# Merging the scores of one attention unit with the outputs of the unit before, and bringing output weights back as whole words

## The chip, the cores and the metric

The kernel runs on one core of a Trainium2 chip. The metric is the device time of one execution in microseconds (us); the median of three runs of the kernel before is 892.08 us. The engines are TensorE (PE in the rows), VectorE (DVE), ScalarE (ACT), GpSimd (POOL) and SyncE (SP), which here only issues transfers.

## The reference

A decayed attention without softmax (retention) is followed by two feed-forward layers over 2304 tokens of width 512:

```python
scores = scale * np.matmul(q, k.transpose(0, 1, 3, 2))     # 4 batches, 8 heads, 576 positions, 64 wide
ret = scores * Dmat                                        # gamma**(i-j) for i >= j, else 0
x = np.matmul(ret, v)                                      # then reshaped to 2304 x 512
h = x @ w_in                                               # 512 -> 2048
x = (h / (1 + np.exp(-1.702 * h))) @ w_out                 # 2048 -> 512
xn = x / np.sqrt(np.mean(x * x, -1) + 1e-6) * rms_g
g = xn @ w_gate                                            # 512 -> 1536
out = (g / (1 + np.exp(-g)) * (xn @ w_val)) @ w_out2       # 1536 -> 512
```

## The kernel before

Every float32 operand of a large matmul is held as two parts: a rounded high part and the remainder, the low part. A product is three matmuls (`three`, L277): high by high, high by low, low by high. The low part of the weight is first needed by the third matmul of each three.

The first feed-forward layer takes the tokens in five blocks of 512, 384, 384, 512 and 512 (blocks 0 to 4), each in 16 steps `f`. A step has an *up* part (`m1_up`, 12 matmuls into a buffer `h`; there are two such buffers, `ps_h`), after which ScalarE applies the activation (L621) and rounds it (L601) and VectorE subtracts to get the low part (L603), and a *down* part (`m1_down`, 12 matmuls into four accumulators). The down part of step `f` is placed two steps later, after the up part of that step (`LAG = 2`, the list `pending`). So TensorE usually sees up(f), down(f-2), up(f+1), down(f-1), and so on.

The attention is computed in units of 128 tokens, 18 of them. Units 0 to 3 come at the start; units 4 to 17 are put between the steps of blocks 0 to 3, in time for the block that needs them. A unit has three phases, each placed in front of an up part: `a_trans` (8 transposes of k and q), `a_scores` (32 small matmuls for the scores, up to 32 for the carried state; 64 by 64 tiles of the array) followed by `a_state` on VectorE, and `a_out` (32 small matmuls for scores by v and up to 32 for the carried state by q; the same tile size). `a_out` leaves its result in two PSUM buffers of the pool `ps_at`; ScalarE copies them (L479), VectorE adds (L483), and the function `parts` is put on the list `rows`. It is run inside the same step's `m1_up`, behind the rounding of the activation: ScalarE rounds x (L489) and GpSimd subtracts (L490).

`attend` also issues the loads of the next unit: the load of unit u+1 is issued at the transposes of unit u (SyncE queue), into the lowest free slots of 512 words (`wslots`). `a_decay` scales v on GpSimd.

The output weights: in block 0 and 1 fourteen of the sixteen rows (`NKEEP = 14`) lie on chip as whole float32 words, and `w_rot` makes the two parts for each step (ScalarE L268, VectorE L269) in one of three buffers. In block 1 both parts are stored to DRAM (512 KB, L272). From block 2 on `w_rot` loads the two parts back, ready for use (512 KB, ScalarE's queue, L274).

Blocks 1 to 4 also carry work for the second layer on ScalarE, VectorE, GpSimd and SyncE (`make`: gate and value weights are joined, combined, split and stored, L189, L190, L243, L834, L861 to L863; sums for the norm). All engines run their instructions in the order in which the program issues them (`manual_schedule`).

Of the kernel before, what the change touches and what calls it, by code (L numbers as in the profile page):

```python
# [24 lines left out]
NSLOT = 22  # L25
# [7 lines left out]
def block_of(t):  # L33

    n = 0
    while t >= BLOCKS[n]:
        t -= BLOCKS[n]
        n += 1
    return n, t
# [3 lines left out]
def kernel(  # L43
# [46 lines left out]
    scrap = dram.tile([1, 16], F32, name="scrap")  # L90
    qrow = dram.tile([1, H * 128], F32, name="qrow")
    srow = dram.tile([1, H], F32, name="srow")
    out_d = dram.tile([NF1, 128, 1024], F32, name="out_d")
    up_d = dram.tile([7 * NF2, 128, 512], F32, name="up_d")


# [61 lines left out]
    def w_free(key, f):  # L158
        give(W.pop((key, f))[0])
# [97 lines left out]
                low() if rest is None else rest.append(low)  # L257

    R = {}

    def w_rot(n, f):


        at = A_ROT + (n * NF1 + f) % 3 * 1024
        both, wh, wl = fast[:, at:at + 1024], fast[:, at:at + 512], fast[:, at + 512:at + 1024]
        if ("out", f) in W:
            w = W["out", f][1]
            nc.scalar.copy(out=wh, in_=w)  # L268
            nc.vector.tensor_tensor(out=wl, in0=w, in1=wh.bitcast(F32), op=ALU.subtract)  # L269
            if n == 1 or f >= NKEEP:  # L270
                w_free("out", f)
                to_store.append(lambda: nc.sync.dma_start(out=out_d[f], in_=both.bitcast(F32)))  # L272
        else:
            nc.scalar.dma_start(out=both.bitcast(F32), in_=out_d[f])  # L274
        R["out", f] = (wh, wl)

    def three(ps, lhs, rhs, first, last, more=False):  # L277
# [38 lines left out]
    def a_tile(u, name):  # L316

        aslots[u, name], t = w_slot() if wfree else half_slot()
        return t

    def a_free(u, *names):
        for nm in names:
            give(aslots.pop((u, nm)))

    def a_load(u, what="kqv"):
        (b, s), (b1, _) = units[u]
        for nm in what:
            t = a_tile(u, nm).rearrange("p (h d) -> p h d", h=H)
            a = {"k": k, "q": q, "v": v}[nm]

            sides = [(slice(0, H), slice(0, H))] if nm == "v" else [
                (slice(j, H, 2), slice(HP * j, HP * j + HP)) for j in range(2)
            ]
            for to, of in sides:
                if b == b1:
                    nc.sync.dma_start(out=t[:, to], in_=a[b, of, s:s + 2 * C, :].rearrange("h p d -> p h d"))
                else:
                    for c, (bc, sc) in enumerate(units[u]):
                        nc.sync.dma_start(
                            out=t[C * c:C * c + C, to], in_=a[bc, of, sc:sc + C, :].rearrange("h p d -> p h d")  # L340
                        )
            raws[u, nm] = t
# [5 lines left out]
    def a_decay(u):  # L348
        vr = raws[u, "v"]
        nc.gpsimd.tensor_tensor(  # L350
            out=vr, in0=vr, in1=vdec.unsqueeze(2).to_broadcast([128, H, D]), op=ALU.mult
        )

    def a_trans(u, where):
        kr, qr = (raws[u, nm] for nm in "kq")
        pt = a_psum(where)

        more = ps_acc.tile([128, 512], F32, tag="acc", name="at") if u == 0 else pt[0]
        for i, t in ((1, kr), (0, qr)):
            for p in range(HP):  # L360
                nc.tensor.transpose(  # L361
                    (more if i == 0 and p > 1 else pt[i])[:, p * 128:(p + 1) * 128],
                    t[:, 2 * p:2 * p + 2, :].rearrange("p h d -> p (h d)"),
                    ident,
                )
        qT = a_tile(u, "qT")
        kT = a_tile(u, "kT")
        nc.scalar.copy(out=kT, in_=pt[1])
        if u > 3:
            nc.vector.tensor_tensor(out=qT, in0=pt[0], in1=qdec, op=ALU.mult)  # L370
        elif u == 0:
            nc.vector.tensor_copy(out=qT[:, :256], in_=pt[0][:, :256])
            nc.scalar.copy(out=qT[:, 256:], in_=more[:, 256:])
        else:
            nc.scalar.copy(out=qT, in_=pt[0])
        if u < 5:
            a_decay(u)
        a_free(u, "q")
        st[u] = tuple(t.rearrange("p (a c) -> p a c", c=128) for t in (qT, kT))
# [4 lines left out]

    def a_scores(u, where):
        qT, kT = st[u]
        sc = a_psum(where)
        for p in range(HP):  # L390
            for c in range(2):
                for j in range(2):
                    hs, cs = slice(64 * j, 64 * j + 64), slice(C * c, C * c + C)
                    nc.tensor.matmul(  # L394
                        sc[j][cs, p * C:(p + 1) * C], kT[hs, p, cs], qT[hs, p, cs], start=True, stop=True
                    )
        kr, vt = raws[u, "k"], raws[u, "v"]
        for p in range(HP):
            for j in range(2):
                for c in range(2):  # L400
                    if goes_on(u, c):
                        hs, cs = slice(64 * j, 64 * j + 64), slice(C * c, C * c + C)
                        nc.tensor.matmul(  # L403
                            sc[c][hs, (HP + p) * D:(HP + p + 1) * D], kr[cs, 2 * p + j, :], vt[cs, head(p, j), :],
                            start=True, stop=True,
                        )
        r = [a_tile(u, f"r{j}").rearrange("p (a c) -> p a c", c=128)[:, :, :C] for j in range(2)]
        for j in range(2):
            nc.vector.tensor_tensor(
                out=r[j], in0=sc[j][:, :HP * C].rearrange("p (a c) -> p a c", c=C),  # L410
                in1=mask.unsqueeze(1).to_broadcast([128, HP, C]), op=ALU.mult,
            )
        st[u] = (qT, r, sc)
        a_free(u, "kT", "k")

    def a_state(u, chunks=(0, 1)):

# [590 lines left out]
    with tc.manual_schedule():  # L1008
# [1 line left out]
        AT = (ps_at.__enter__(), "at")  # L1010
        ACC = (ps_acc, "acc")

        per_block = {}
        for u in range(len(units)):
            per_block.setdefault(block_of(2 * C * u)[0], []).append(u)
        phases = [(fn, u) for n in range(1, N1) for u in per_block[n] for fn in (a_trans, a_scores, a_out)]

        to_load = [("in", 0), ("in", 1)]
        for f in range(NF1):
# [178 lines left out]
        load()  # L1198
        late = list(range(6, len(units)))

        def attend(phases):
            for fn, u in phases:
                fn(u, AT)
                if fn is a_out and u + 1 < len(units):
                    a_decay(u + 1)
                if fn is a_scores:
                    a_state(u)
                if fn is a_trans and u > 4 and late:
                    a_load(late.pop(0))

        pending, spread = [], []

        def run(todo, k):
            for _ in range(min(k, len(todo))):
                todo.pop(0)()
# [16 lines left out]
        own = NSLOT - 13  # L1232
        x = None
        for n in range(N1):
            todo = [t for t in phases if t[1] in per_block.get(n + 1, [])]
            gap = {}
            for i, t in enumerate(todo):
                at = 1 + i * (NF1 - 2) // max(1, len(todo))
                gap.setdefault((2, 3, 5, 6, 8, 10, 11, 12, 14)[i] if n == 0 else at, []).append(t)
            last = n == N1 - 1  # L1240
            if n == 2:
                assert not set(range(own, own + 2)) - set(wfree), wfree
# [15 lines left out]
                FILL["parts"] = wslots[:, 14 * TH:20 * TH]  # L1258
            for f in range(NF1):
                if n == 0:  # L1260
                    attend(gap.get(f, []))
                    if f == 2:
                        conv_next(2)
                    if f > 0:
                        w_rot(n, f - 1)
                    if f > 1:
                        conv_next(2)
                if n == 1 and f == 0:
                    nc.sync.dma_start(out=rg, in_=rms_g.rearrange("(k p) -> p k", p=128))
                if n == 1 and f == 11:  # L1270
                    w_rot(n, f - 1)
                    assert wfree[-11:] == list(range(own + 2, NSLOT)), wfree
                    del wfree[-11:]
                    FILL["made"] = [wslots[:, i * 512:i * 512 + 512] for i in range(own + 6, own + 1, -1)]
                    FILL["sums"] = wslots[:, (NSLOT - 6) * 512:(NSLOT - 4) * 512]
                    FILL["gate"], FILL["val"] = (wslots[:, (NSLOT - i) * 512:(NSLOT - i + 1) * 512] for i in (4, 3))
                    sfree.append(NSTG)
# [21 lines left out]
                if n == 1 and 0 < f < NKEEP + 1 and f != 11:  # L1299
                    w_rot(n, f - 1)  # L1300
                if n > 0:
                    attend(gap.get(f, []))
                    if n > 1 or f >= NKEEP:
                        w_rot(n, f)
                if (n, f) == (0, 0):


                    m1_up(n, f, lambda: conv_join([to_conv.pop(0)]), lambda: conv_words(*to_conv[0]))
                else:
                    m1_up(n, f, lambda: run(rows, 1))  # L1310
                run(to_store, len(to_store))
                if norm:
                    spread = norm.popleft() + spread
# [20 lines left out]
                w_rot(n, NF1 - 1)  # L1334
        run(to_store, len(to_store))
        assert not made and not parts_of
        run(down(pending.pop(0)), KD)
        sfree.extend((NSTG + 1, NSTG + 2))
        chunks = []
# [124 lines left out]
```

## Time and profile before

| | |
|---|---|
| runs | 891.97, 892.08, 892.97 us (median 892.08) |
| the profiled execution's own time | 893.62 us |
| its span in the profile | 891.5 us (2.1 us lie around it) |
| TensorE busy | 882.4 us, 99% of the span, 6170 matmuls |
| VectorE, ScalarE, GpSimd busy | 509.9, 384.4, 83.8 us |
| transfers | 192.96 MB, mean 216 GB/s |

A wait of TensorE lengthens the execution one for one while TensorE is the engine that is never idle; the other engines' idle time costs nothing by itself. Matmuls are pipelined: the time that one takes is read from the distance of the starts, not from its own length.

### The profile page before, as it was taken

The numbers are of one execution on the slowest core, as the hardware profiler recorded it, in microseconds if no ns is written. First come the engines' busy times: TensorE is split into PE (matmuls) and PEld (weight loads), VectorE is DVE, ScalarE is ACT, GpSimd is POOL, SyncE is SP. The second block draws the span as 40 slices with busy tenths as digits, with TensorE's granted clock in tenths as the row PEclk, the third lists the DMA queues.
The fourth block names the chain that finished last, engine by engine and source line by source line (L and its number), as shares of the span: only waits on it lengthen the run. The fifth ranks groups of instructions, "written<-read, shape, count | busy, mean of one in ns | idle before, by whom it ended". The sixth has DMA issues, their size and how long they took to land.

```text
span 891.5 us, 16172 instructions
## 1 busy us (share of the span) xinstructions
PE 882.4 (99%) x6170; PEld 794.1 (89%) x6170; DVE 509.9 (57%) x920; ACT 384.4 (43%) x767; POOL 83.8 (9%) x95
## 2 busy tenths in 40 slices
PE   8999999999999999999999999999999999999998
PEld 7788889999999888888889999999999999999997
DVE  4787644454584457445744557766565666344444
ACT  3796644365545534454453344334323215122222
POOL 2200101122232212211200000000000000000000
PEclk9999999999999999999999999999999999999999
DMA  9985435489999976779597676557655556555553
GB/s 221 266 262 186 131 117 191 145 267 330 301 294 319 289 238 196 277 275 330 205 312 267 207 263 212 167 155 238 223 153 157 155 157 219 175 157 163 166 165 106
DMA packets 153131, 192.96 MB, mean 216 GB/s; under 512 B 66204, under 2 KB 94112, under 8 KB 153056
## 3 DMA queue, kind: packets, MB, share of 16 engines
q1 hardware_dynamic: 145268, 165.32, 59.4%
q10 hardware_dynamic: 7660, 26.36, 8.8%
q8 instruction: 49, 0.80, 0.3%
q0 software_dynamic: 128, 0.27, 0.2%
q14 instruction: 26, 0.21, 0.1%
HBM read 149.70 MB, written 42.21 MB: 215 GB/s over the span
## 4 chain that ended last, share of the span: by engine, by line
PE 97%; DVE 1%; ACT 1%; DMA 0%; issue 0%; SPq 0%; DVEq 0%; ACTq 0%
PE h L280 18%; PE h L282 17%; PE h L281 17%; PE acc L281 11%; PE acc L282 11%; PE acc L280 11%; PE v L282 2%; PE v L281 2%; PE v L280 2%; PE at L361 2%; PE at L470 2%; PE at L394 1%; PE at L403 1%; PE at L506 1%; DMA wslots<-in_q_dram 0%; PE at L563 0%
## 5 line engine op out<-in xcount | busy, mean ns | idle before, releaser
L280 PE MATMUL h<-fast 128*128 128x384 f32 (+1 forms) x824 | 291.5, 354 | 1.6 <-DVE S L535 1.1
L282 PE MATMUL h<-fast 128*128 128x384 f32 (+1 forms) x824 | 287.3, 349 | 0.0
L281 PE MATMUL h<-fast 128*128 128x384 f32 (+1 forms) x824 | 286.9, 348 | 0.1
L911 DVE TENSOR_TENSOR wslots<-h,wslots 128x384 f32<-128x384 f32 x180 | 100.2, 557 | 151.3 <-PE h L282 151.0
L282 PE MATMUL acc<-fast 128*128 128x512 f32 (+1 forms) x464 | 174.4, 376 | 0.0
L281 PE MATMUL acc<-fast 128*128 128x512 f32 (+1 forms) x464 | 174.2, 375 | 0.0
L280 PE MATMUL acc<-fast 128*128 128x512 f32 (+1 forms) x464 | 173.5, 374 | 0.0
L280 PEld LDWEIGHTS h<-fast 128*128 128x128 f32 x824 | 154.7, 188 | 13.2 <-ACT fast L215 1.5
L281 PEld LDWEIGHTS h<-fast 128*128 128x128 f32 x824 | 154.8, 188 | 9.0 <-issue 0.3
L282 PEld LDWEIGHTS h<-fast 128*128 128x128 f32 x824 | 154.6, 188 | 7.7
L603 DVE TENSOR_TENSOR fast<-g,fast 128x512 fp32r<-128x512 f32 (+1 forms) x80 | 56.2, 703 | 123.8 <-ACT fast L601 123.6
L944 ACT CAST fast<-g 128x384 fp32r<-128x384 f32 x36 | 18.6, 517 | 220.4 <-DVE g L914 220.4
L621 ACT ACTIVATE g<-h 128x512 f32<-128x512 f32 (+1 forms) x80 | 44.4, 555 | 142.9 <-PE h L282 140.3
L282 PEld LDWEIGHTS acc<-fast 128*128 128x128 f32 x464 | 87.1, 188 | 13.2
L281 PEld LDWEIGHTS acc<-fast 128*128 128x128 f32 x464 | 87.1, 188 | 12.1
L280 PEld LDWEIGHTS acc<-fast 128*128 128x128 f32 x464 | 87.1, 188 | 12.0
L601 ACT CAST fast<-g 128x512 fp32r<-128x512 f32 (+1 forms) x80 | 46.4, 580 | 2.5
L834 POOL TENSOR_TENSOR wslots<-wslots 128x256 f32<-128x256 f32 x48 | 40.3, 860 | 74.2 <-DVE wslots L243 54.3
L862 DVE TENSOR_TENSOR wslots<-wslots 128x256 fp32r<-128x256 f32 x84 | 39.7, 502 | 13.1 <-ACT wslots L861 12.9
L189 ACT ACTIVATE sslots<-sslots 128x512 f32<-128x512 f32 x55 | 37.0, 674 | 4.8 <-DMA sslots<-in_moe_w_gate_dram 4.6
L190 ACT ACTIVATE sslots<-sslots 128x512 uint32<-128x512 uint8 x55 | 36.5, 663 | 0.0
L861 ACT CAST wslots<-wslots 128x256 fp32r<-128x256 f32 x84 | 30.8, 401 | 11.9 <-DVE wslots L243 8.6
(136 smaller groups left out, 857.4 us busy)
## 6 DMA issues: line engine op xcount, KB each, us to landing
fast<-up_d SPq DMA_DIRECT2D x252, 256.0 KB, 3.1
fast<-out_d ACTq DMA_DIRECT2D x50, 512.0 KB, 5.5
up_d<-wslots SPq DMA_DIRECT2D x84, 256.0 KB, 5.1
sslots<-in_moe_w_out_dram SPq DMA_DIRECT2D x20, 512.0 KB, 5.3
out_d<-fast SPq DMA_DIRECT2D x16, 512.0 KB, 3.8
sslots<-in_moe_w_in_dram SPq DMA_DIRECT2D x15, 512.0 KB, 5.2
sslots<-in_moe_w_gate_dram SPq DMA_DIRECT2D x11, 512.0 KB, 6.4
sslots<-in_moe_w_val_dram SPq DMA_DIRECT2D x10, 512.0 KB, 7.0
```

What stands on the lines that cost most here:

```text
L189: nc.scalar.activation(out=hi, in_=hi, func=AF.Prelu, scale=2.0 ** -112, alpha=-(2.0 ** 32))
L190: nc.scalar.activation(out=lo, in_=byte, func=AF.Copy, scale=1 / 32, bias=-31 / 64)
L280: nc.tensor.matmul(ps, lh, rh, start=first, stop=False, skip_group_check=more)
L281: nc.tensor.matmul(ps, lh, rl, start=False, stop=False, skip_group_check=more)
L282: nc.tensor.matmul(ps, ll, rh, start=False, stop=last, skip_group_check=more)
L601: nc.scalar.copy(out=gh, in_=g)
L603: nc.vector.tensor_tensor(out=gl, in0=g, in1=gh.bitcast(F32), op=ALU.subtract)
L621: nc.scalar.activation(out=g, in_=ps, func=AF.Gelu_apprx_sigmoid)
L834: nc.gpsimd.tensor_tensor(out=o, in0=a, in1=b, op=op)
L861: nc.scalar.copy(out=wh.bitcast(F32R), in_=w)
L862: nc.vector.tensor_tensor(out=wl.bitcast(F32R), in0=w, in1=wh, op=ALU.subtract)
L911: nc.vector.tensor_tensor(out=o, in0=a, in1=b, op=ALU.add)
```

## The change

- The scores of unit u and the outputs of unit u-1 become one phase, `a_both`, for units 8 to 17. The outputs then go to the two buffers of `ps_h` instead of `ps_at`. A step with such a phase is *joined*: the down part that would follow the up part is put in front of it. `a_decay` of unit u moves to its transposes, the load of unit u+1 to `a_both` of unit u.
- The places of the phases are written out by hand (`at_steps`). Joined steps are 4, 7, 10 of block 1; 2, 6, 10, 14 of block 2; 3, 7, 9 of block 3.
- Of the fourteen kept output weights the whole word is stored in block 1 (256 KB, straight from its slot, without waiting for the parts). From block 2 on the word is loaded (256 KB) and halved on chip by `w_halve`, called behind `m1_up`: in step f it halves the weight of step f-1.

```diff
+    def w_halve(f=-1):
+        while whole and whole[0][0] != f:
+            _, wh, wl = whole.popleft()
+            nc.scalar.copy(out=wh, in_=wl.bitcast(F32))
+            nc.vector.tensor_tensor(out=wl, in0=wl.bitcast(F32), in1=wh.bitcast(F32), op=ALU.subtract)
...
-            if n == 1 or f >= NKEEP:
+            if f >= NKEEP:
                 w_free("out", f)
-                to_store.append(lambda: nc.sync.dma_start(out=out_d[f], in_=both.bitcast(F32)))
+                to_store.append(lambda: nc.sync.dma_start(out=both_d[f - NKEEP], in_=both.bitcast(F32)))
+            elif n == 1:
+                nc.sync.dma_start(out=out_d[f], in_=w)
+                w_free("out", f)
+        elif f >= NKEEP:
+            nc.scalar.dma_start(out=both.bitcast(F32), in_=both_d[f - NKEEP])
         else:
-            nc.scalar.dma_start(out=both.bitcast(F32), in_=out_d[f])
+            nc.scalar.dma_start(out=wl.bitcast(F32), in_=out_d[f])
+            whole.append((f, wh, wl))
...
-        if u < 5:
+        if u < 5 or u > 7:
             a_decay(u)
...
+        def a_both(u, where):
+            a_scores(u, where, True)
+            a_out(u - 1, HID)
+            a_state(u)
...
+        phases += [(a_trans, 7), (a_scores, 7)]
+        phases += [(fn, u) for u in range(8, len(units)) for fn in (a_trans, a_both)]
+        phases.append((a_out, len(units) - 1))
+        at_steps = (
+            (2, 3, 5, 6, 8, 10, 11, 12, 14),
+            (0, 1, 2, 4, 5, 7, 8, 10),
+            (0, 2, 4, 6, 8, 10, 12, 14),
+            (1, 3, 5, 7, 9, 11, 13),
+        )
...
+            if late and (fn is a_both or fn is a_trans and 4 < u < 8):
+                a_load(late.pop(0))
+            return fn is a_both
...
+                if joined:
+                    run(down(pending.pop(0)), KD)
                 if (n, f) == (0, 0):
...
                     m1_up(n, f, lambda: run(rows, 1))
+                w_halve(f)
                 run(to_store, len(to_store))
```

## Rows read from the trace of the kernel before

**Rows 1.** The page, busy time of the engines (us, share of the span, instructions).

```profile
PE 882.4 (99%) x6170; PEld 794.1 (89%) x6170; DVE 509.9 (57%) x920; ACT 384.4 (43%) x767; POOL 83.8 (9%) x95
```

**Rows 2.** Busy time by stretch: blocks 2 and 3, with granted clock and DMA share.

```profile
201.50:282.80 81.30, 81.30 (x900) 78.12 (x900) 51.16 (x99) 42.07 (x95) 23.61 (x24) 1.00 0.98 309
282.80:372.30 89.50, 89.50 (x868) 74.04 (x867) 49.81 (x94) 42.18 (x89) 18.27 (x19) 1.00 0.79 248
```

**Rows 3.** Timeline of TensorE, steps of 384 columns (start, duration, line, operation).

```profile
197.35 0.33 PE L280 MATMUL acc<-fast 128*128 128x384 f32 x1
...
201.51 0.33 PE L280 MATMUL acc<-fast 128*128 128x384 f32 x1
...
206.55 0.33 PE L280 MATMUL acc<-fast 128*128 128x384 f32 x1
...
208.73 0.69 PE L394 MATMUL at<-wslots 64*64 64x64 f32 x32
209.24 0.65 PE L403 MATMUL at<-wslots 64*64 64x64 f32 x32
...
212.01 0.33 PE L280 MATMUL acc<-fast 128*128 128x384 f32 x1
...
264.40 0.33 PE L280 MATMUL acc<-fast 128*128 128x384 f32 x1
...
267.09 0.41 PE L470 MATMUL at<-wslots,S 64*64 64x64 f32 x16
...
269.63 0.33 PE L280 MATMUL acc<-fast 128*128 128x384 f32 x1
```

**Rows 4.** Timeline of TensorE, a step of 512 columns.

```profile
380.44 0.39 PE L280 MATMUL h<-fast 128*128 128x512 f32 x1
...
383.16 0.39 PE L280 MATMUL acc<-fast 128*128 128x512 f32 x1
```

**Rows 5.** Timeline of four engines behind the up part after unit 7's outputs.

```profile
141.20 0.69 DVE L269 TENSOR_TENSOR fast<-wslots,fast 128x512 fp32r<-128x512 f32 x1
...
144.87 0.33 PE L280 MATMUL acc<-fast 128*128 128x384 f32 x1
...
145.07 0.49 ACT L621 ACTIVATE g<-h 128x384 f32<-128x384 f32 x1 [1.57 <-PE h L282]
...
146.02 0.62 ACT L489 CAST fast<-x 128x512 fp32r<-128x512 f32 x1
...
146.54 0.62 ACT L268 CAST fast<-wslots 128x512 fp32r<-128x512 f32 x1
...
146.71 1.28 POOL L490 TENSOR_TENSOR fast<-x,fast 128x512 fp32r<-128x512 f32 x1 [12.46 <-ACT fast L489]
...
147.19 1.35 DVE L269 TENSOR_TENSOR fast<-wslots,fast 128x512 fp32r<-128x512 f32 x1 [0.49 <-ACT fast L268]
```

**Rows 6.** Timeline of ScalarE and GpSimd at the same place in block 3.

```profile
301.68 0.60 ACT L621 ACTIVATE g<-h 128x512 f32<-128x512 f32 x1 [2.29 <-PE h L282]
...
303.53 1.30 POOL L490 TENSOR_TENSOR fast<-x,fast 128x512 fp32r<-128x512 f32 x1 [8.34 <-ACT fast L489]
```

**Rows 7.** Timeline of ScalarE and VectorE: evacuating the outputs of units 7 and 12.

```profile
142.85 0.65 ACT L479 COPY x<-at 128x256 f32<-128x256 f32 x2 [1.68 <-PE at L470]
143.60 0.49 DVE L483 TENSOR_TENSOR x<-at,x 128x128 f32<-128x128 f32 x2 [1.71 <-ACT x L479]
...
251.83 0.38 ACT L479 COPY x<-at 128x256 f32<-128x256 f32 x1 [1.53 <-PE at L470]
...
254.41 0.48 DVE L483 TENSOR_TENSOR x<-at,x 128x128 f32<-128x128 f32 x2
```

**Rows 8.** SyncE's queue and landing times: the load of unit 9 (KB each, us to landing).

```profile
142.34 1.66 SPq L336 DMA_DIRECT2D wslots<-in_k_dram  x2
144.10 1.55 SPq L336 DMA_DIRECT2D wslots<-in_q_dram  x2
...
wslots<-in_q_dram SPq DMA_DIRECT2D x2, 128.0 KB, 4.4
```

More of the change, by code (lines that the diff above doesn't have):

```diff
@@ L92 @@
     srow = dram.tile([1, H], F32, name="srow")
-    out_d = dram.tile([NF1, 128, 1024], F32, name="out_d")
+    out_d = dram.tile([NKEEP, 128, 512], F32, name="out_d")
+    both_d = dram.tile([NF1 - NKEEP, 128, 1024], F32, name="both_d")
     up_d = dram.tile([7 * NF2, 128, 512], F32, name="up_d")
@@ L259 @@
     R = {}
+    whole = deque()
+    def w_halve(f=-1):
[3 more added lines that the diff above has]
+            nc.vector.tensor_tensor(out=wl, in0=wl.bitcast(F32), in1=wh.bitcast(F32), op=ALU.subtract)
     def w_rot(n, f):
@@ L383, in goes_on, with a_scores @@
         return units[u][c][1] + C < S
-    def a_scores(u, where):
+    def a_scores(u, where, over=False):
         qT, kT = st[u]
@@ L406, in a_scores @@
                         )
+        if over:
+            a_free(u, "kT", "k")
         r = [a_tile(u, f"r{j}").rearrange("p (a c) -> p a c", c=128)[:, :, :C] for j in range(2)]
@@ L413, in a_scores @@
         st[u] = (qT, r, sc)
-        a_free(u, "kT", "k")
+        if not over:
+            a_free(u, "kT", "k")
     def a_state(u, chunks=(0, 1)):
@@ L1011 @@
         ACC = (ps_acc, "acc")
[L1013 to L1016, printed above, removed]
+        HID = (ps_h, "h")
+        def a_both(u, where):
+            a_scores(u, where, True)
+            a_out(u - 1, HID)
+            a_state(u)
+        phases = [(fn, u) for u in range(4, 7) for fn in (a_trans, a_scores, a_out)]
+        phases += [(a_trans, 7), (a_scores, 7)]
+        phases += [(fn, u) for u in range(8, len(units)) for fn in (a_trans, a_both)]
+        phases.append((a_out, len(units) - 1))
+        at_steps = (
[4 rows of a table added]
+        )
+        gap = {(n, f): phases.pop(0) for n, steps in enumerate(at_steps) for f in steps}
+        assert not phases
         to_load = [("in", 0), ("in", 1)]
@@ L1199, with attend @@
         late = list(range(6, len(units)))
[L1201 to L1209, printed above, removed]
+        def attend(n, f):
+            if (n, f) not in gap:
+                return False
+            fn, u = gap[n, f]
+            fn(u, AT)
+            if fn is a_out and u < 7:
+                a_decay(u + 1)
+            if fn is a_scores:
+                a_state(u)
+            if late and (fn is a_both or fn is a_trans and 4 < u < 8):
+                a_load(late.pop(0))
+            return fn is a_both
         pending, spread = [], []
@@ L1234 @@
         for n in range(N1):
[L1235 to L1239, printed above, removed]
             last = n == N1 - 1
@@ L1260 @@
                 if n == 0:
-                    attend(gap.get(f, []))
+                    joined = attend(n, f)
                     if f == 2:
@@ L1271 @@
                     w_rot(n, f - 1)
-                    assert wfree[-11:] == list(range(own + 2, NSLOT)), wfree
+                    assert wfree[-11:] == list(range(own + 2, NSLOT)), (wfree, aslots, [(k, W[k][0]) for k in W if k[0] == "out"])
                     del wfree[-11:]
@@ L1301 @@
                 if n > 0:
-                    attend(gap.get(f, []))
+                    joined = attend(n, f)
                     if n > 1 or f >= NKEEP:
                         w_rot(n, f)
+                if joined:
+                    run(down(pending.pop(0)), KD)
                 if (n, f) == (0, 0):
@@ L1336 @@
         assert not made and not parts_of
+        w_halve()
         run(down(pending.pop(0)), KD)
```

## The prediction

> **What bounds the kernel.** I read the page first: TensorE is busy 99% of the span [rows 1]. The table by stretch shows that in blocks 2 and 3, where most of the change lies, TensorE has no idle time at all, at a granted clock of 1.00, while VectorE is busy 51 of 81 us and ScalarE 42, and the DMA engines are nearly full in block 2 (share 0.98) [rows 2]. So time can only be saved by giving TensorE less to do, and any new wait of TensorE is paid in full. Fewer bytes or less work elsewhere are worth nothing by themselves. Then I read TensorE's timeline, for what a phase costs between two steps, and the timelines of the other engines behind one up part, for when a product of theirs is ready.
>
> **Part 1: ten phases fewer.** Two plain steps, 12 up and 12 down matmuls, take 201.51 - 197.35 = 4.16 us. With a scores phase of 64 small matmuls between, the same stretch takes 212.01 - 206.55 = 5.46: the phase costs 1.30. Unit 13's outputs have 48 small matmuls (32 and the 16 of the row): 269.63 - 264.40 = 5.23, so 1.07 [rows 3]. Sixteen small matmuls are 0.23, 64 are 0.92, and 0.38 us is a fixed cost of going into and out of a phase of 64 by 64 tiles. `a_both` has the same matmuls as the two phases that it replaces, in one tile size, so it saves one fixed cost: 10 units, 3.8 us. The other bound is 0, if 128 small matmuls in a row run slower than 64; no row has so many. I take 3.8, since L403's 32 begin 0.51 us after the first of the scores' 32, 16 ns for each, with nothing lost between the two [rows 3].
>
> **Part 2: halving on chip, in ordinary steps.** 42 weights (14 in each of three blocks) get a ScalarE copy and a VectorE subtract. The nearest rows are the same operations on the same shapes in block 1: 0.62 us (L268) and 0.69 us (L269) [rows 5]. In an ordinary step the halving of weight f-1 stands behind up(f), and down(f-1) comes after down(f-2) and up(f+1), 4.16 us later or 5.44 in the wider blocks: cost nothing, hidden by these two. 26 and 29 us more on ScalarE and VectorE fit into their idle time [rows 2].
>
> **Part 3: halving in a joined step.** Here the cover is gone. Down(f-2) has been put in front of up(f), so after up(f) TensorE goes straight to up(f+1) and then to down(f-1). Between the end of up(f) and the first use of weight f-1 lies one up part: 2.08 us at 384 columns (half of 4.16), 2.72 at 512 (383.16 - 380.44 [rows 4]). The low part is needed by the third matmul, two twelfths of a part later: 2.43 and 3.17 us after the end of up(f).
>
> When is it ready? Behind up(f) ScalarE has, in order, the activation, its rounding, the rounding of x (L489, because the outputs of a unit were made in this very step), and only then the copy of `w_halve`. Block 1 of the kernel before shows exactly this row of work. Up ends where the next dense matmul starts, 144.87; the activation starts at 145.07, the rounding of x at 146.02, the copy L268 runs from 146.54 to 147.16, and VectorE's L269 starts at 147.19. But it takes 1.35 us instead of 0.69, because GpSimd's L490, released by the rounding of x, runs from 146.71 to 147.99; L269 ends 0.55 us behind it, at 148.54 [rows 5]. So the low part is ready 148.54 - 144.87 = 3.67 us after the end of up(f). In the kernel before that cost nothing, for its use was further off.
>
> In block 2 TensorE then waits 3.67 - 2.43 = 1.24 us in each of four joined steps. In block 3 the activation starts at 301.68, so up ended 0.20 before, at 301.48, and GpSimd starts at 303.53, 2.05 us after the end against 146.71 - 144.87 = 1.84: everything is 0.21 later [rows 5, 6]. 3.88 - 3.17 = 0.71 us in each of three. The sum is 4 x 1.24 + 3 x 0.71 = 7.1 us. The lower bound is that VectorE is not held up by GpSimd: ready 0.66 earlier, so 0.58 and 0.05, sum 2.5. An upper bound of 9 adds some 0.27 each for a chain that starts late. Block 1's joined steps have no halving behind the up part.
>
> On the hold-up, the Trainium skill says under "Who interferes with whom" on the page "SBUF — State Buffer" that VectorE with two SBUF inputs and a GpSimd instruction that reads SBUF exclude each other, and that the one that issues first wins. The row agrees (1.35 against 0.69, ending behind GpSimd). By the rule a VectorE that issues first would bring the sum to the lower bound; the rows have GpSimd first, by 147.19 - 146.71 = 0.48 us.
>
> **Part 4: outputs in the up buffers.** Up(f) needs the buffer that VectorE's add of L483 reads last. For unit 7 the add ends at 144.09, 1.24 us after the copies began [rows 7], and the down part put in front covers 2.08. For unit 12 it is 254.89 - 251.83 = 3.06 us, since VectorE was behind: 1.0 us over the cover [rows 7]. Of the four joined steps in block 2 I count half of one such case: 0.5 us, with bounds 0 and 4.
>
> **Part 5: loads issued later.** In block 1 the load of units 9 and 10 is now issued at the end of the joined phase, and the transposes stand one step later. By the order in which slots are freed, k takes the slot of the transposed q of the unit whose outputs were just made, so it can't start before the phase ends. Cover: one down, one up and four transposes of k, some 4.6 us. Unit 9's load before took from 142.34 to the second issue of q, about 144.88, plus 4.4: 6.9 us [rows 8]. So a wait of up to 2.3 us each; but half the bytes of the weights' stores are gone and the queue is free by then. I take 0.5 each, 1.0 in all, bounds 0 and 4.6. In blocks 2 and 3 two steps, at least 8.3 us, cover 6.9.
>
> **At nothing:** the whole-word stores wait for no parts, but a slot is now free only when its store has read it; units 7, 9 and 10 get such a slot for a tile first used two steps later, some 8 us. The decay of v on GpSimd comes two steps ahead of its use. 42 x 256 KB less to load shortens no wait that TensorE has.
>
> **Sum.** -3.8 + 7.1 + 0.5 + 1.0 = +4.8 us. Against the profiled execution's 893.62 that is 898.4; the median of the runs is 1.54 lower, so 896.9 us.
>
> **Rivals.** (a) The saving stays, and the kernel is faster. Mechanism: the rounding of x is not ahead of the halving in the joined step. Then the copy starts where L489 did, 146.02 - 144.87 = 1.15 us after up, and the low part is there at about 2.5: 0.1 over in block 2, nothing in block 3. It decides below 2.43 us. With loads in time: 892.1 - 3.8 + 0.4 + 0.5 = 889.2. For it: ScalarE is idle half the time in block 2 [rows 2]. Against it: the code runs x's rounding in the same step's up part. 0.13.
>
> (b) VectorE is not held up: -3.8 + 2.5 + 0.5 + 1.0 = +0.2, 892.3, no change. For it: GpSimd is only 0.48 us ahead. Against: L269 in rows 5. 0.17.
>
> (c) A second wait beside the halving: loads at their bound give 3.6 more, 900.5; evacuation at its bound 3.5 more, 900.4; a merged phase that saves nothing 3.8 more, 900.7. 0.10 together. For evacuation the Trainium skill, "TensorEngine Tiling (Array Packing)", section "PSUM Bottleneck", warns that small tiles speed up the matmuls and not the emptying of PSUM, which may become the limit. By that rule the time is the 900.4 of this case; of four outputs in block 2 one was late.
>
> **Numbers.** My forecast, the wait for the halved weight in seven joined steps, has 0.60 and gives 896.9. A measurement of this kernel tells about 0.2%, 1.8 us, from no change. Faster is (a) and a little of (b): 0.14. Same is most of (b) and the edge of the forecast: 0.16. Slower is the rest: 0.70. The range leaves out (a) and the upper half of (c): 890.8 to 900.5; the forecast's own, with its unknown waits, is 894 to 900.
>
> **What would show it.** In the profile after, TensorE should wait 7 times, in front of the third or first matmul of a down part into `acc`, for VectorE at the subtract of `w_halve`, 1.2 us each in block 2 and 0.7 in block 3; none in block 4, which has halving but no joined steps. A phase of 128 small matmuls should cost 2.2 us. Waits of the transposes of units 9 and 10 for k or q, or of an up part for L483 in a joined step, would show parts 4 and 5. I am wrong if VectorE's subtract ends within 2.4 us of the up part, or if phases cost the same merged.

## The result, and the profile after

The kernel is slower by a little under 1%: 900.49 us (median of 4 runs, 899.66 to 901.69) against 892.53 (4 runs), ratio 1.0085 with a 95% interval of 1.0072 to 1.0099. The profiled execution has a span of 899.3 us. One place in the description of the change has to be put right: by `at_steps` the joined steps of block 3 are 3, 7 and 11, not 3, 7 and 9. There are three of them either way, all with a weight to halve.

First the page of the changed kernel: busy times, the shares of the chain that ended last, and the group of third matmuls of the down parts. The last line is the same group in the kernel before.

```profile
PE 880.9 (98%) x6170; PEld 791.2 (88%) x6170; DVE 540.9 (60%) x962; ACT 404.3 (45%) x809; POOL 89.0 (10%) x95
...
PE 90%; ACT 3%; DVE 3%; DMA 2%; issue 1%; SPq 0%; POOL 0%; ACTq 0%; DVEq 0%; POOLq 0%
...
L297 PE MATMUL acc<-fast 128*128 128x512 f32 (+1 forms) x464 | 175.1, 377 | 4.3 <-DVE fast L268 4.3
...
L282 PE MATMUL acc<-fast 128*128 128x512 f32 (+1 forms) x464 | 174.4, 376 | 0.0
```

TensorE has the same 6170 matmuls as in [rows 1] and is busy 1.5 us less, yet the span is 7.8 us longer: the time went into waits. L297 is the third matmul of `three` in the changed file (L282 before, where it never waited); L268 is the subtract of `w_halve`. The table of TensorE's waits names them (in total, times, longest):

```profile
PE acc L297 <- DVE fast L268: 4.3, 6, 0.8
PE h L751 <- DVE fast L734: 2.2, 2, 1.9
...
PE h L295 <- DMA fast<-up_d: 0.9, 1, 0.9
PE at L376 <- DMA wslots<-in_q_dram: 0.7, 2, 0.6
...
PE h L295 <- DVE x L501: 0.4, 1, 0.4
```

The table counts only the time in which TensorE was empty. What a wait costs is read from the starts. This is a joined step of block 2 in the changed kernel, its 128 small matmuls and then the first use of the halved weight, in the timeline of four engines:

```profile
207.44 0.33 PE L295 MATMUL acc<-fast 128*128 128x384 f32 x1
...
209.62 0.69 PE L409 MATMUL at<-wslots 64*64 64x64 f32 x32
...
211.06 0.65 PE L488 MATMUL at<-wslots,S 64*64 64x64 f32 x32
...
213.83 0.33 PE L295 MATMUL h<-fast 128*128 128x384 f32 x1
...
217.05 0.62 ACT L507 CAST fast<-x 128x512 fp32r<-128x512 f32 x1
...
217.57 0.61 ACT L267 CAST fast<-fast 128x512 fp32r<-128x512 f32 x1
...
217.75 1.29 POOL L508 TENSOR_TENSOR fast<-x,fast 128x512 fp32r<-128x512 f32 x1 [9.69 <-ACT fast L507]
...
218.22 1.36 DVE L268 TENSOR_TENSOR fast<-fast 128x512 fp32r<-128x512 f32 x1 [0.48 <-ACT fast L267]
...
218.24 0.44 PE L295 MATMUL acc<-fast 128*128 128x384 f32 x1
...
218.52 0.33 PE L296 MATMUL acc<-fast 128*128 128x384 f32 x1
...
219.64 0.45 PE L297 MATMUL acc<-fast 128*128 128x384 f32 x1 [0.79 <-DVE fast L268]
...
219.92 0.34 PE L295 MATMUL acc<-fast 128*128 128x384 f32 x1
```

Two down parts and the phase between them take 213.83 - 207.44 = 6.39 us, 2.23 more than the 4.16 of two plain parts: a merged phase costs 2.23 us, where two phases cost 1.30 each [rows 3]. So 0.37 us per merged phase is saved, 3.7 in all. Added up over all of them, the starts say the same: 21 phases of units 7 to 17 take 26.8 us before, the 11 that are left take 23.1. Then the up part that began at 213.83 ends 2.08 later, at 215.91, a second up part follows at once, and the down part should begin at 217.99. It begins at 218.24, waiting for the high part; its third matmul, due 0.35 us after 217.99, comes at 219.64, for VectorE's subtract ended at 219.58, 3.67 us after the end of the up part. The third begins 0.06 us after the subtract's end, and the matmul behind it comes 0.28 us later instead of 0.17. The two parts together take 1.4 us more than they would.

The same chain in step 3 of block 3, where the up part ends at 310.45 and the subtract at 312.98 + 1.36 = 314.34, 3.89 us later; this one costs 0.86 us:

```profile
310.45 0.39 PE L295 MATMUL h<-fast 128*128 128x512 f32 x1
...
312.98 1.36 DVE L268 TENSOR_TENSOR fast<-fast 128x512 fp32r<-128x512 f32 x1 [0.35 <-ACT fast L267]
...
314.39 0.50 PE L297 MATMUL acc<-fast 128*128 128x512 f32 x1 [0.59 <-DVE fast L268]
```

The second row of the table of waits was not foreseen. In block 3 the joined step 7 has no wait at the halving, since TensorE waits somewhere else before it, in the sums of the norm (two matmuls against a matrix of ones, L750 and L751). The timeline there:

```profile
338.31 1.29 POOL L508 TENSOR_TENSOR fast<-x,fast 128x512 fp32r<-128x512 f32 x1 [19.27 <-ACT fast L507]
...
338.79 1.36 DVE L268 TENSOR_TENSOR fast<-fast 128x512 fp32r<-128x512 f32 x1 [0.35 <-ACT fast L267]
...
338.98 0.33 PE L750 MATMUL h<-fast,ones 128*128 128x384 f32 x1
...
340.07 1.08 DVE L734 TENSOR_TENSOR fast<-ssq,fast 128x384 fp32r<-128x384 f32 x1
...
341.20 0.44 PE L751 MATMUL h<-fast,ones 128*128 128x384 f32 x1 [1.89 <-DVE fast L734]
```

GpSimd's subtract holds up the halving's subtract, and that the low part of the norm's sum, which stands behind it on VectorE; the second matmul of the sums comes 2.2 us after the first instead of 0.2. The low part of the sum (L734) itself takes 1.08 us here, beside GpSimd's next instruction, against 0.55 at the sums of block 2 in the same run.

The whole stretch of the first layer, from the up part that waits for the carried state near the start to the first up part of the second layer, leaves out the start, which differs from execution to execution (that up part begins anywhere from 29.8 to 33.6 us). It took 470.57 - 31.88 = 438.7 us before and 477.81 - 30.82 = 447.0 after: 8.3 longer. By the distances of the starts: phases -3.7; halving 4 x 1.4 + 2 x 0.86 = 7.3; sums 2.7; unit 10's q 0.7; an evacuation 0.6; together 7.6. The other 0.7 is not assigned; a halving 0.2 late in an ordinary step is part of it.

### The profile page after: what moved, and what is told of

Its sections match the earlier page's. It is cut to its first block, busy times and chain, and to the rows that moved or that the text cites. A ratio compares the mean times of both kernels' runs of the same rounds, so it can differ in the third digit from the quotient of the medians.

```text
span 899.3 us, 16209 instructions
## 1 busy us (share of the span) xinstructions
PE 880.9 (98%) x6170; PEld 791.2 (88%) x6170; DVE 540.9 (60%) x962; ACT 404.3 (45%) x809; POOL 89.0 (10%) x95
## 4 chain that ended last, share of the span: by engine, by line
PE 90%; ACT 3%; DVE 3%; DMA 2%; issue 1%; SPq 0%; POOL 0%; ACTq 0%; DVEq 0%; POOLq 0%
PE h L295 16%; PE h L297 16%; PE h L296 16%; PE acc L297 11%; PE acc L295 10%; PE acc L296 10%; PE v L297 2%; PE v L296 2%; PE v L295 2%; PE at L376 1%; PE at L488 1%; DMA fast<-up_d 1%; DVE fast L268 1%; PE at L409 1%; PE at L418 1%
## 5 line engine op out<-in xcount | busy, mean ns | idle before, releaser
L297 PE MATMUL h<-fast 128*128 128x384 f32 (+1 forms) x824 | 287.2, 349 | 0.0
L297 PE MATMUL acc<-fast 128*128 128x512 f32 (+1 forms) x464 | 175.1, 377 | 4.3 <-DVE fast L268 4.3
L297 PEld LDWEIGHTS h<-fast 128*128 128x128 f32 x824 | 154.7, 188 | 7.7
L297 PEld LDWEIGHTS acc<-fast 128*128 128x128 f32 x464 | 87.1, 188 | 20.1 <-DVE fast L268 6.8
L852 POOL TENSOR_TENSOR wslots<-wslots 128x256 f32<-128x256 f32 x48 | 44.7, 950 | 79.7 <-DVE wslots L244 59.8
L880 DVE TENSOR_TENSOR wslots<-wslots 128x256 fp32r<-128x256 f32 x84 | 36.7, 467 | 6.5 <-ACT wslots L879 6.3
L508 POOL TENSOR_TENSOR fast<-x,fast 128x512 fp32r<-128x512 f32 x14 | 18.3, 1304 | 222.3 <-ACT fast L507 222.3
L268 DVE TENSOR_TENSOR fast<-fast 128x512 fp32r<-128x512 f32 x42 | 38.0, 904 | 3.3 <-ACT fast L267 3.3
```

What stands on the lines that cost most here:

```text
L268: nc.vector.tensor_tensor(out=wl, in0=wl.bitcast(F32), in1=wh.bitcast(F32), op=ALU.subtract)
L297: nc.tensor.matmul(ps, ll, rh, start=False, stop=last, skip_group_check=more)
L852: nc.gpsimd.tensor_tensor(out=o, in0=a, in1=b, op=op)
L880: nc.vector.tensor_tensor(out=wl.bitcast(F32R), in0=w, in1=wh, op=ALU.subtract)
```

## The experiments

Each ratio is to runs of the kernel before that were taken beside the run, whose medians lie between 892.0 and 892.6 us. The last column is from one profiled execution each; where its mean granted clock was under 0.999 it stands beside it, and a part of the length is then that of the lower clock.

| run | us (median, runs) | ratio to the kernel before (95%) | first layer's stretch, us |
|---|---|---|---|
| before | 892.53 (4) | | 438.7 |
| changed | 900.49 (4) | 1.0085 (1.0072 to 1.0099) | 447.0 |
| e1 merged phases, no halving | 892.91 (12) | 1.0007 (0.9991 to 1.0023) | 438.6 |
| e2 halving, phases as before | 893.28 (12) | 1.0005 (0.9994 to 1.0017) | 438.9 |
| e3 halving first in joined steps | 893.02 (12) | 1.0000 (0.9988 to 1.0012) | 440.1 |
| e4 x's subtract issued later | 902.34 (4) | 1.0106 (1.0081 to 1.0132) | 449.2 (clock 0.996) |
| e5 e3, sums and unit 10 moved | 891.92 (12) | 0.9995 (0.9982 to 1.0007) | 438.4 (clock 0.997) |
| e6 x's subtract on VectorE, later | 895.81 (4) | 1.0041 (1.0026 to 1.0055) | 441.7 |
| e7 down part behind again | 905.08 (4) | 1.0140 (1.0127 to 1.0153) | 450.2 (clock 0.998) |
| e8 halving before x | 895.45 (4) | 1.0033 (1.0020 to 1.0046) | 442.1 |
| e9 e5, halving first everywhere | 890.78 (12) | 0.9985 (0.9973 to 0.9998) | 437.9 |
| e10 e1, sums and unit 10 moved | 891.01 (12) | 0.9987 (0.9973 to 1.0001) | 438.6 |

The theory: in joined steps the cover between the halving and its use (the work of TensorE that stands between the two) is one part instead of two, and the weight is late. Rivals: halving costs wherever it stands; merging itself costs.

**e1: merged phases alone.** `w_rot` as in the kernel before, so both parts are stored and loaded.

```diff
-            nc.scalar.dma_start(out=wl.bitcast(F32), in_=out_d[f])
-            whole.append((f, wh, wl))
+            nc.scalar.dma_start(out=both.bitcast(F32), in_=out_d[f])
```

> The changed kernel, but both parts of the output weights are stored and loaded back as in the kernel before; no halving on chip. If the late halved weight is the cause (theory): the saving of ten phases (3.7 us) stays and only the late load of unit 10 (0.7) and one late evacuation (0.5) stand against it, so 2.5 us under the kernel before, ratio 0.997. Rival, merging itself costs (down part in front, outputs in the up buffers, later loads): still 4 us or more over it. Rival, halving costs wherever it stands: also faster than before, so the next run has to tell it from the theory.

The 8 us are gone, so the rival that merging itself costs 4 us or more is out (the interval ends at 2 us). But the kernel is not faster than before: the expectation of 0.997 was a miss. Its waits in the first layer, from the table of waits:

```profile
PE acc L288 <- ACT fast L276: 1.4, 1, 1.4
...
PE h L744 <- DVE fast L727: 0.8, 1, 0.8
PE at L369 <- DMA wslots<-in_q_dram: 0.3, 1, 0.3
```

2.5 us of waits, which with the pipeline's refilling come to some 3.4 by the starts, where the kernel before has no wait of TensorE in that stretch. So the saving is there and new small waits eat it: the norm's sums, as in the changed kernel, a load, and one of 1.4 us at the end of block 1, where the rounding of a weight (L276) stands on ScalarE behind the first gate weights, for which ScalarE waited 5.4 us.

GpSimd has a share in the wait at the sums here too, without any halving. The subtract for the sums (L727) starts just behind GpSimd's subtract for x and takes 1.66 us instead of 0.55; with 0.55 it would have ended at 333.01, before the matmul that waits for it was due, at 333.26:

```profile
332.42 1.29 POOL L501 TENSOR_TENSOR fast<-x,fast 128x512 fp32r<-128x512 f32 x1 [18.94 <-ACT fast L500]
...
332.46 1.66 DVE L727 TENSOR_TENSOR fast<-ssq,fast 128x384 fp32r<-128x384 f32 x1
```

**e2: halving alone.** The kernel before with the whole words, and `w_halve(f)` behind `m1_up`.

```diff
                     m1_up(n, f, lambda: run(rows, 1))
+                w_halve(f)
```

> The kernel before, with its phases as they were, but the fourteen kept weights return as whole words and are halved on chip behind each up part. Theory: no joined steps, two parts of cover, so no change: ratio 0.999 to 1.001 and no wait of TensorE at the halving. Rival, halving loads ScalarE, VectorE and GpSimd's shared time so that it costs wherever it stands: 4 us or more over the kernel before, ratio 1.005.

No change, as expected, and no wait of TensorE in the first layer. 42 copies and subtracts cost nothing that the runs can tell (the interval ends at 1.5 us) under two parts of cover. The rival that halving costs 4 us or more wherever it stands is out.

**e3: halving first in joined steps.**

```diff
                 if joined:
+                    w_halve(f)
                     run(down(pending.pop(0)), KD)
```

> The changed kernel with one line more: in a joined step the waiting weight is halved before the down and up part of that step, not behind the up part. Theory: the seven waits at the halving go, and with them the wait of the norm's sums in block 3, which came from VectorE held up behind the same subtract; 10 us under the changed kernel, some 890 us, ratio to the kernel before 0.997. Rival, the transfer of the weight is not there yet so early and ScalarE waits for it in front of the activation: the gain is lost in waits for the activation, 895 us or more.

The waits of the joined steps are gone (the 0.5 us left at L268 stand in an ordinary step) and the time falls by 7.5 us: the theory holds. But it is level with the kernel before, not 3 us under it. Its waits in the first layer:

```profile
PE h L751 <- DVE fast L734: 1.9, 2, 1.1
PE at L376 <- DMA wslots<-in_q_dram: 1.0, 1, 1.0
PE acc L297 <- DVE fast L268: 0.5, 1, 0.5
...
PE h L295 <- DVE x L501: 0.4, 1, 0.4
```

The sums still wait; I had put that wait down to the halving's subtract alone, which was wrong, for e1 has it too without any halving. The step after a joined one begins with its up part at once, and that takes a part of cover from whatever was laid out for the step. The wait at the sums is longer with halving (1.9 us here, 2.2 in the changed kernel) than without (0.8 in e1), and with halving in unjoined steps there is none (e2).

**e4: x's low part issued one step later on GpSimd.**

```diff
             nc.scalar.copy(out=xh, in_=x)
-            nc.gpsimd.tensor_tensor(out=xl, in0=x, in1=xh.bitcast(F32), op=ALU.subtract)
+            rows.append(lambda: nc.gpsimd.tensor_tensor(out=xl, in0=x, in1=xh.bitcast(F32), op=ALU.subtract))
```

> The changed kernel, but GpSimd's subtract for x is issued one step later, so it doesn't stand beside the halving in a joined step. If VectorE's subtract is held up by GpSimd: the halved weight is there 0.66 us earlier, the waits in block 2 fall from 1.4 to about 0.75 and those in block 3 from 0.85 to 0.2, 4 us less in all, some 896.5 us, and the subtract takes 0.69 us. If the subtract takes 1.35 us for another reason (both operands in one buffer, for example): no change, 900 us.

No gain (1.0106, with an interval that overlaps the changed kernel's), because the experiment didn't do what it was meant to. The place in the program was another, but GpSimd had nothing in between: it had been idle for 7.89 us, the rounding of x ended at 220.25 + 0.62 = 220.87, and the subtract started 0.07 us later:

```profile
220.25 0.62 ACT L507 CAST fast<-x 128x512 fp32r<-128x512 f32 x1
...
220.94 1.29 POOL L508 TENSOR_TENSOR fast<-x,fast 128x512 fp32r<-128x512 f32 x1 [7.89 <-ACT fast L507]
...
221.42 1.36 DVE L268 TENSOR_TENSOR fast<-fast 128x512 fp32r<-128x512 f32 x1 [0.48 <-ACT fast L267]
```

**e6: x's low part on VectorE, one step later.** What e4 was meant to do, with `nc.vector` in place of `nc.gpsimd`.

> The changed kernel, but x's low part is subtracted by VectorE one step later and GpSimd has no part in it. The run with GpSimd's subtract issued later changed nothing, because an idle GpSimd took it at once. If the two engines exclude each other: the halving's subtract takes 0.69 us, the waits fall by 0.66 each to about 0.75 in block 2 and 0.2 in block 3, some 896 us. If the subtract is slow by itself: 1.35 us again and 900 us.

Confirmed: 895.8 us against the 896 expected. The halving's subtract takes 0.69 us, and the third matmul comes 0.45 us behind the second, where it came 1.12 behind it in the changed kernel. In this row the decay of the next v starts on GpSimd in the same instant, and now it is the one that is long (1.59 us against 1.04 in most of this run):

```profile
217.54 0.69 DVE L268 TENSOR_TENSOR fast<-fast 128x512 fp32r<-128x512 f32 x1 [0.48 <-ACT fast L267]
...
217.54 1.59 POOL L365 TENSOR_TENSOR wslots<-wslots,vdec 128x512 f32<-128x512 f32 x1 [8.77 <-PE h L297]
...
217.84 0.34 PE L296 MATMUL acc<-fast 128*128 128x384 f32 x1
...
218.29 0.44 PE L297 MATMUL acc<-fast 128*128 128x384 f32 x1
```

Three of the four waits in block 2 now cost 0.75 us by the starts, as expected. That the total fits so well is in part chance: the wait at the sums fell too (from 2.2 to 0.7 us), and one evacuation came 0.5 us later, neither of which the expectation had.

**e8: x rounded behind the halving.** The mechanism of rival (a).

```diff
-                    m1_up(n, f, lambda: run(rows, 1))
+                    m1_up(n, f, lambda: None if joined else run(rows, 1))
                 w_halve(f)
+                if joined:
+                    run(rows, 1)
```

> The changed kernel, but in joined steps x is rounded behind the halving instead of before it, so ScalarE has the copy 0.5 us sooner and VectorE is ahead of GpSimd. Theory: the low part is there 2.5 us after the up part, the wait is 0.1 to 0.3 in block 2 and none in block 3: 6 us less, some 894 us. Rival, the weight's transfer or VectorE's backlog is what is late: waits as before.

895.5 us against the 894 expected. The subtract now runs ahead of GpSimd and ends 217.13 + 0.69 = 217.82; the third matmul comes at 217.88:

```profile
217.13 0.69 DVE L268 TENSOR_TENSOR fast<-fast 128x512 fp32r<-128x512 f32 x1
...
217.69 1.29 POOL L508 TENSOR_TENSOR fast<-x,fast 128x512 fp32r<-128x512 f32 x1 [10.21 <-ACT fast L507]
...
217.88 0.44 PE L297 MATMUL acc<-fast 128*128 128x384 f32 x1
```

The waits at the halving fall from 4.3 to 0.7 us, all of it in ordinary steps, and those at the sums rise from 2.2 to 2.9. The order of one rounding on ScalarE is worth 5 us; e6 takes out the other half of the same chain and gains as much.

That two engines exclude each other here is what the Trainium skill says on "SBUF — State Buffer", "Who interferes with whom": the one that issues first has the shared port, whatever the shapes. The three runs agree: 1.36 us behind GpSimd (e4), 0.69 beside or ahead of it (e6, e8). In one joined step of e6 the subtract took 0.97 us, and there the decay of v was already running on GpSimd when it began.

**e7: the down part behind the up part in joined steps.** The two lines `if joined: run(down(...), KD)` are left out.

> The changed kernel, but in joined steps the down part stays behind the up part. Theory: with two parts of cover the waits at the halving vanish, but the up part now waits for the emptying of its buffers, about 1.3 us in each of ten joined steps and near 3 in the one where VectorE is behind: 14 us more for 7 to 9 less, some 905 us. Rival, the order of the down part has nothing to do with the halving's wait: both waits, 914 us.

905.1 us, as expected. The halving has its cover back and no wait is left there; instead the up part waits in all ten joined steps for VectorE's add or ScalarE's copy out of its buffers:

```profile
PE h L295 <- DVE x L501: 12.0, 8, 2.7
PE h L295 <- ACT x L497: 1.3, 2, 0.8
```

So putting the down part in front is right for the buffers and wrong for the weight: one part of cover was moved from one to the other.

**e5: e3, with the sums one step later and unit 10's transposes one step later.**

```diff
-                    norm = deque([[], []] + [[op] for op in sq[:5]])
-                    cuts = (5, 9, 13, 15, 18, 21) if n == 2 else (5, 9, 13, 17, 21)
+                    norm = deque([[], []] + [[op] for op in sq[:5]] + [[]])
+                    cuts = (5, 9, 13, 17, 21)
...
-            (0, 1, 2, 4, 5, 7, 8, 10),
+            (0, 1, 2, 4, 5, 7, 9, 10),
```

> The third run (halving first in joined steps) with two more places moved: the norm's sums of blocks 2 and 3 come one step later, away from the step behind a joined one, and the transposes of unit 10 stand one step later, so that its load has two steps. If what eats the saving of ten phases in the third run are these small waits (sums 2.2 us, load 0.7 to 1.0): 3 us under the kernel before, 889.5 us, ratio 0.9965, with no wait of TensorE over 0.6 us after block 0. Rival, the saving of a merged phase is not 0.37 us each but near nothing: ratio 1.000 and the step times show it.

The line for `cuts` does one thing more than move the sums: the later instructions of the norm in block 2 come in four groups instead of five.

The sums don't wait any more, although their subtract takes 1.66 us again in block 3: its use is now a step further off. A miss all the same: the ratio is 0.9995, for a new wait of 1.7 us has come, at a weight halved behind an ordinary up part while VectorE was behind with the norm's steps, which now fall into that place. Unit 10's load is in time, but the load of unit 15, in block 3, is 0.8 late.

Why VectorE was behind can be read from the rows. From 259.33 to 266.18 GpSimd works without a break, and VectorE's instructions in that time take longer: 0.98 us for L768, which takes 0.56 at 267.82, and 1.52 for the halving's subtract instead of 0.69. It is the same pattern as in the changed kernel, here with GpSimd's work for the second layer (L852) and the decay of v (264.83 to 266.18) as well as the subtract for x:

```profile
260.90 3.96 POOL L852 TENSOR_TENSOR wslots<-wslots 128x256 f32<-128x256 f32 x4
...
262.40 0.98 DVE L768 TENSOR_TENSOR t<-t,m 128x384 f32<-128x384 f32 x1
...
265.20 1.52 DVE L268 TENSOR_TENSOR fast<-fast 128x512 fp32r<-128x512 f32 x1
...
266.78 0.44 PE L297 MATMUL acc<-fast 128*128 128x384 f32 x1 [1.66 <-DVE fast L268]
```

**e9: e5, halving first in every step of blocks 2 to 4.**

```diff
+                w_halve(f)
                 if joined:
-                    w_halve(f)
                     run(down(pending.pop(0)), KD)
...
                     m1_up(n, f, lambda: run(rows, 1))
-                w_halve(f)
```

> The fifth run, but the halving stands before the down and up part in every step of blocks 2 to 4, not only in joined ones. In the fifth run one wait of 1.8 us was left, at a weight halved behind the up part that follows a joined step, where VectorE was behind with the norm. If that is all that stood in the way, it goes: the stretch from the first up part that waits for the carried state to the end of the first layer takes some 436 us against 438.7 before, and the kernel some 889.5 us, ratio 0.997. Rival: the weight's transfer is too late for ScalarE in ordinary steps and the activation waits: no gain, ratio 1.000 or over.

The lowest time of all: 890.78 us, 0.15% under the kernel before and 1% under the changed one. The interval (0.9973 to 0.9998) is just clear of 1, so the saving is at the edge of what these runs can tell. It misses the 889.5 us and the 436 us that were expected (the stretch took 437.9), since the wait at the halving became shorter but didn't go. 2.2 us of waits are left in the first layer:

```profile
PE acc L297 <- DVE fast L268: 1.3, 2, 1.0
PE at L376 <- DMA wslots<-in_q_dram: 0.9, 1, 0.9
```

**e10: e1 with the same two places moved.**

> The first run (merged phases, both parts loaded, no halving on chip) with the norm's sums one step later and the transposes of unit 10 one step later. Its waits were 1.4 us for a weight's rounding in block 1, 0.9 for the sums, 0.4 for a load: the last two go, so some 437 us for the same stretch, ratio 0.998. If it comes out like the ninth run, halving on chip is worth nothing once it is hidden; if 2 us slower, the whole-word store is worth that.

0.9987 (0.9973 to 1.0001), not to be told from e9. The sums and unit 10's load don't wait any more, but the stretch took 438.6 us and not 437: the wait of 1.2 us for a rounding in block 1 is still there, and a new one of 1.6 us has come for the load of unit 15. Whether the whole words are worth anything by themselves stays open: the two medians differ by 0.2 us, and each ratio is known to some 1.2 us.

## Why the prediction was right

Forecast were 896.9 us, slower, with a range of 890.8 to 900.5. Measured were 900.49. The sign and the mechanism of the main term were right, but the size was not: 8.0 us slower instead of 4.8. That 900.49 still lies in the range, by 0.01 us, is luck. It is above the forecast's own band (894 to 900), and the upper end was the price of another case, rival (c) with two late loads, which didn't come. The five terms of the sum came out well: -3.7 + 7.3 + 0.6 + 0.7 = 4.9 us for 4.8. What failed is that the sum had no term for the norm's sums.

- *Part 1, 3.8 us saved.* 2.23 us for a merged phase against the 2.2 forecast: 3.7 us. Right.
- *Part 2, nothing in ordinary steps.* Right by e2.
- *Part 3, 7.1 us in seven joined steps.* The low part was ready 3.67 us after the up part in block 2, to the hundredth what the rows of block 1 gave, and 314.34 - 310.45 = 3.89 in block 3 against 3.88. The third matmul comes 0.05 to 0.06 us behind it, and the next one is 0.11 late. With these two, which the sum left out, a wait cost 1.4 and 0.86 us instead of 1.24 and 0.71. The seventh wait was covered by that of the sums. 7.3 us in place of 7.1, and e3, e6, e7 and e8 take it away, each in the way that the chain says. (e7 gives the time back at the buffers.)
- *Part 4, 0.5 us.* 0.6, in one joined step of block 2, at unit 12's outputs, the same that were late before [rows 7]; e7 shows 13.3 us of waits that the down part in front covers.
- *Part 5, 1.0 us.* 0.7, at unit 10 alone.
- *What the sum lacked.* The norm's sums, 2.7 us. The rule of part 3, that the step behind a joined one has lost a part of cover, holds for everything that is laid out by steps; I applied it to the weight only. That the sums stood one step behind joined steps could be read in the code. Rival (c) had a second wait beside the halving, with 0.10, but none of its three places was this one. Some 0.7 us within the first layer and 0.6 behind it, where TensorE waits 0.9 us for a load of the second layer's weights, are not explained further; the start of the profiled execution was 1.1 us shorter than before.

Rivals (a) and (b) would have been 889 and 892 us; e8 and e6 show that their mechanisms work (the waits at the halving fall from 4.3 to 0.7 and 0.6 us), and that the kernel didn't meet their conditions. The times of e8 and e6, 895.5 and 895.8, lie above both prices, in part because neither price had the sums.

## What to carry to other kernels

Cover is counted in parts of the engine that never idles: when one of its parts is moved forward, list everything that was placed by the old order (weights, sums, buffers, loads) and count again what stands between each product and its use. A saving of 0.4 us per phase on a full engine is easily eaten by waits of a few tenths at other places, so the profile's table of waits has to be nearly empty before it shows. Count GpSimd's instructions too: in these runs a VectorE subtract that starts behind one of them takes 1.36 to 1.66 us instead of 0.55 to 0.69, and that was part of the wait for the weight and of those that the later runs met. Where a chain of the same instructions already runs in another stretch with slack, its rows give the ready time of the new chain directly.

## What the runs showed that was not expected

Issuing GpSimd's subtract later in the program did nothing, since GpSimd was idle (e4: it started 0.07 to 0.08 us after its input in either version). And the start of the kernel varies by as much as the ten phases are worth (3.7 us): the up part that waits for the carried state began at 29.83 us in one profiled execution and at 33.55 in another, and no run shows why, so effects under 4 us were read from a stretch that leaves the start out.
